# A convolution and joint network on one core: tap 0 loaded in halves of rows, a turned sample block copied out by two engines, the last group's lower rows stored in two column halves

## The chip, the cores and the metric

The kernel runs on one core of a Trainium2 chip. The metric is device time in microseconds (us): the median of several executions. One further execution was taken with the hardware profiler; every start and duration below is from it, counted from the first instruction of its span.

The core's engines, as the profile names them: PE (matrix products; PEld loads the weights of a product), DVE and ACT (vector and activation engine, which also copy results out of PSUM), POOL, and SP, which does no arithmetic and issues most DMA transfers. ACT issues a few. A "q" behind a name (SPq) means the engine's sequencer, which waits and issues.

## The reference

```python
# x (2, 4000, 512)  w1, w2 (5, 512, 512)  g (2, 8, 512)  w_f, w_g, w_o (512, 512), all bf16
def reference(x, w1, w2, g, w_f, w_g, w_o):
    B, T, D = x.shape
    K = w1.shape[0]
    pad = K // 2
    xp = jnp.pad(x, ((0,0),(pad,pad),(0,0)))
    h = jnp.zeros_like(x)
    for i in range(K):
        h = h + jnp.einsum("btc,cd->btd", xp[:, i:i+T, :], w1[i])
    h = _gelu(h)[:, ::2, :]
    ...                                  # the same again with w2: f, (2, 1000, 512)
    fe = jnp.einsum("btd,de->bte", f, w_f)
    ge = jnp.einsum("bud,de->bue", g, w_g)
    j = jnp.tanh(fe[:, :, None, :] + ge[:, None, :, :])
    return jnp.einsum("btud,dv->btuv", j, w_o)      # (2, 1000, 8, 512)
```

Two convolutions of five taps over time, each followed by gelu and by dropping every second sample; then a product with w_f, a sum with each of eight vectors per batch entry, tanh, and a product with w_o that gives 16,000 rows of 512.

## The kernel before

**Layout.** Channels lie on the 128 partitions in four chunks (index k, or c for the chunk of an input channel and m for the chunk of an output channel), samples along the free dimension. The samples of `x` lie in memory the other way round (a sample's 512 channels side by side), so they must be turned.

**Order of work.** Every operation (a group of matmuls, a copy, a DMA) is recorded in a plan, with the tiles that it reads and writes. Which engine does it, and in which order each engine does its own, stands in the strings of `ORDER`, written out by hand: two characters are one operation's number. `Plan.emit` then puts in the waits that the tiles demand. The numbers `cost`, `wire` and `nbytes` are a planner's estimates and change nothing in the program that runs. Each engine, SP too, works through its list strictly in order, so a waiting instruction holds all behind it.

**The first stage, up to about 23 us.** The outputs of the first convolution for the first 396 kept samples of batch entry 0 are computed directly, tap by tap, while the rest of the input is still on its way:
- `load_xr` (line 438) loads the first samples in two blocks, `xr[0]` of 128 rows and `xr[1]` of 72, each row holding four consecutive samples.
- `load_w1` (lines 430 and 456) loads the taps of w1. Taps 0 and 4 come in column halves `h` (output channels 0 to 255, and 256 to 511), taps 2, 1 and 3 whole. The order on SP is tap 0 first half, tap 4 first half, tap 0 second half, tap 4 second half, tap 2, tap 1, tap 3. A `gate` makes SP wait with a load until an earlier one has landed: tap 4's second half waits for `xr[0]`, tap 2 for `xr[1]`, tap 1 for the first half of tap 4, tap 3 for the second half of tap 4. Behind them on SP stand the transposing loads `load_x6` (line 445) of the other samples into `xq` and `xp`.
- While the loads run, PE does eight products with zeros (`warm_mm`). Then it turns the two blocks (line 489): for each block `rt` and each parity `pp` of the samples eight transposes into one PSUM bank, 4, 6, 5 and 7 in PE's order. DVE copies the banks of block 0 into `xs[0]` (line 496), ACT those of block 1 (line 404). On DVE the copy of the odd samples stands behind three sums over w1.
- `direct` (product of line 412) does, for a tap and an output chunk m, four matmuls, one for each input chunk k. The columns are 2 × 198 samples. The output chunks gather in PSUM banks 0 to 3. Taps go in the order 0, 4, 2, 1, 3; taps 0, 4 and 2 read even samples, taps 1 and 3 odd ones.
- `w1part` (DVE lines 398 and 500, ACT line 404) forms sums of taps, chunk by chunk of the outputs, for the units below. The first three on DVE read taps 0 and 4, the next tap 2. The tiles are `ssum`, `w_x` and `w_t`. In between, DVE and ACT form sums of samples (`row`) from `xq`.

**The units.** The rest of both convolutions goes in `Triple`s and `Unit`s: three outputs side by side from nine products of sums. Their first products are mixed into tap 3 of the direct stage on PE: the first output chunk of tap 3, then the first product of unit 1 (tile `row`, made by DVE, times `w_x`), the second chunk of tap 3, and so on.

**The joint stage.** After the convolutions, `Seven` handles four blocks of 128 output rows by seven products of half-size blocks in place of eight (`p1` to `p7`). Results gather in a tile `og` of four blocks by 512 columns: blocks 0 and 1 are the upper rows, 2 and 3 the lower. `block(r, c)` is half r of the rows and half c of the columns, 256 columns wide. Block (1, 1) is written by DVE in `p7`, block (1, 0) by ACT in `p4`, the upper blocks by DVE in `p2` and `p3`. `stores(r)` (line 932) stores both column halves of rows r in one DMA on SP, 256 KB in rows of 1 KB.

**The end.** For the last group, PE's order is p7, p2, p3, then the single block that is left over (`Plain`, two column halves of 64 KB, stored from ACT, line 830), then p4. On SP the last three issues are: the lower rows of the group before, the upper rows of the last group, its lower rows. Then SP waits for all stores.

Of the kernel before, what the change touches and what calls it, by code (L numbers as in the profile page):

```python
# [12 lines left out]
P = 128  # L13
# [50 lines left out]
class Op:  # L64
# [6 lines left out]
        "0Y0Z0a0b0c0d0e0f0g0i0k0m0u0v0w0x0y0z0_0-1011121314151617182D191h2d1A2w1B2K2L2n2o1j1k2f2g2F2G2y2z2q2r2N37382O34353P2k"  # L71
        "3Q313K2l3I323L3Y3u3V3i3j3W3S3f3T423w3a3b433x4Z4B4D4E4L3-3g45464M3l3m4b4c4O404I4p4g4m5M4J4j4k4P4n4w4x5W4z4r4_5q5X4s4h"
        "5O5P5T5U505s6M515_5Z5t5-6m6W6X5a6O6w6x6P6T5x5y7B796U61626o6p7J7K6Z7C7U6t7S6z6a7G7c7q7M6u7V7d7H7N6_7Z7s7t7f7g8U7a7_84"
        "817-827x8B8C8E7y86878F8n8e8o8s8W8H8X8f8b8I8u8v908p8q919E8h8z8c8_9G9H9L939R8i9S9M9U9V949g9O9p9P9r9i9w9zA49yA1A8AAAOA3"
        "9kAF9lAjAkAaAbACAIB2AxAyAJALB3AgBEAhBWBFAqAdArBXAeB8B9BZBLBMAMB5BaB6BlAtAuBcBdBSBTBrBBBOBsBCBPCIBfBuBvCCCFCGBgC9CAC2"
        "CDC3CmCUBiCJBjCVCLB_B-CbCpCqCXCYCnCcCMD6D7CsCvCtDGDKCfDLCwD3CgD4DWDdDCCyDeDXDNDODDDQDyDRDvCzDzDoDwDkDgDhDlDpDTDUEFEC"
        "EDE5EUE6E2D-EVE3EPE0EQEaEbEGEgELEuE-EvEMFDEXEYEdEeFEF0FPF3ExFGFHEyF5FJFsFtFkFXFyFRFMFYFKFaFbFzFNG8G9FvFwGLFgFhFmGMG2"
        "GBGCGFF-GGG0GUGOGZGVGRGSGfGuGgGPGXGoGvH1GiGpH4GjGxH2H6GyG_HZG-HNHCHyHTHOHzHDHUHFHGHbHhHiHQHWHXHqHRIZHrHJH-I0HKI2I3IC"
        "HkHlITIaIyIDI5IUIJI6IzIKIcIWIFIjIXIGIkJ2J3IdJPImJCJQJDIsJ5I-ItInJ0JJJ6JSJKJTJuJvJfJYJFJgJVJGJiJjJWJ_JZK8J-K9JxK1K2KN"
        "JyKTKUKOJoKFKWKGJpKXK_KQKBKCKdKeLLKmKRKuKvLRK-LMKnKxKgKhLSL8L9L1LFL2KyLULbLqLVLcLGLrLOLPLkLBLCMPLlMQMJMKLtM4LeLfM5Lz"  # L80
        "LuL_LwMmLxMnMZMaMMMSM7MNMBM8MTMCMpMsMtMqMgMhNHN0MvMcN1NIMdMwNmN3N4N7NKN8NNNLNnNONQNXNYOFNROGNaNsNeNfNbNvO0O1NtNpNqNw"
        "OVOWOLOMOOOiO3OjO4OPOIOJOoOyOzOpOrO7O8OsOlOmOcOYPCOdOZPFP9PAPGPDP3P4PIPaO-P0PbPSPPPQPJQ1PTQ2PjPkPgPdPhPePqPrPWPXQDQE"
        "PtQ4Q5PuPxPyQ7Q8QGQKQLQHQAQBQNQOQRQYQUQV"),
    "act": (
        "080l1M0n1p1O1z1S1r1R2T1Q2E1i2e1t1-1C1D1b2p2M1l1d1E1G2x1F2V392P2s2Y362X3R2Z2j2m3J3Z2J3v3C3k3o3U3E3X3330444C3p3q3h3O4N"
        "4a473n4T413e4q5N4l4Q3_4V4K4o544-5Y554i535r4v4y4H526N66604f6n5V706y5L6Y5b5S686V5w5K7A5z5p7L636S727T6b715o6L6v7e7I5i7O"
        "7k6s6-7r7w857h7Y6l7F807m8D7b6K838V7z8G8O8t8P6E8g6k8Q8J988A6e8a78929F8d8j9K8r8-9T9A959N9W8y9q9h9Q9j9_A59sAUA0APA7AVCk"
        "AlAHAEAWCiAKAYAXAZBGAsB1BNANBAC7B0C5BYBmBtC6BwA-CBClC4DJCWCjC8CZDICoDtDHDMDuD5F9ChETESDY9oC_FpDiFBCPF7F8FADsE7EEERFr"
        "EHEhEwGKFFFQF4EzFoFqGtGsFZFcFCHvGAFnHuG3INGJIwGhGYIRH5GkGwJNHwHPHEIQHHHxH_IPJsKrI4ISIEIVIxI_IOIbIlKsJEJRIoLoJOJwJhJk"
        "JtJXKLKAKVKJKqKKKfKMKwNiL0KiLTLALJLKLsLdMkMLLpM6KtLyMoMbMHM9MuMIMlMeNJNFNkNDNPN5NoNZOHNcNENlOXNjO5NGO_OhODOaOEPBOgP1"  # L90
        "PRPcPHQ3PUPsPiQFPvQ9QIQSQTQWQa"),
    "dve": (
        "000h1J1K1n0j1L1P1o1x1N1y1m1v1q2R1I2S1T1s1V1w1U1_1W1X1H1Y1Z1a1c1u202h1e2H2Q2_2U2-1f2I1g2i2W2u2a2c2b3M2t3N2v3D3A3B3r3c"
        "3F3d3G3y3z3s3H4F4G3t49484d4R4U4e4A4S4X564Y4W4t4u585d5e5Q57645c5F5u655H5I675v5R6B746c5l5G6Q6A5m5J6R6q6r6C6H69737D6I7E"
        "5j6D5h7R5k5g5n7Q757P7W7X6F6d6h7u7l7v6i776G7j6J7i6f7p887n6g897o6j8R8T8Y8S768w8Z8m8l978x96999I9X9b9J8k9f9Y9d9a9Z9B9t9u"
        "9x9v9-A29eABA6A99CAG9mAcAD9n9DAzA_B4AiAoAmAnATBHBpBIApAfBbB7AvBeBnBUBQBDBqC-CQBhCECHCKBkC0CrCdCNCODZDaEAD8CuEqDbCxDf"
        "DEDPDSD_DxDmDqDVEBDrEiEjElEWE4E1EcEnFTEoENEZF1EfFIF6EpFlFuFSFLFOF_FxFiGNGDGHG1GaGTGQI8HAH9HdGWGqH7GzH0HaH3HVHcHjHYHS"
        "HsHLI1HmI9IgJ8I7ILIYIHJ9IhJ4IeIuJ1J7JUJbK5JcJHJLJaK0K3JzKPKHJqKYKDKSKbL5M0KcLNKoLXL7KzLWLHLQLDL3LmLgLvL-MyM2MVM3MRMD"
        "MOMiMrN2MUMxN9NMNTNyNVNUORNzNSNgNrO2NxOkNuONOKOQO9OqOeOnPEP5OtPNOxPLPmPMPKPfPlPYQ6PzQMQCQPQZ"),
    "pool": (  # L100
        "010203040522210o0p0q0r0s0t5f8N9cASBJAQARBKCSBoD0D2CRD1CTDcErE8EsEtE9EkG4FUEmFWGbG6G5GcFVH8G7GdHeGeHgHBJAIAHfIfIiIBJB"
        "JdK4K7JeKZL4KaK6M1LYL6LZLaMXMWMzMYM_M-OSN_NWOTN-OuOUOvOwPnPOPoPp"),
    "sp": (
        "0607090A0B0C0D0E0F0G0H0I0J0K0L0M0N0O0P0Q0R0S0T0U0V0W0X232425262728292A2B2C595A5B5C5D5E8K8L8MAwBRBVBxByBzC1CaCeD9DADB"
        "DFDjDnEIEJEKEOE_F2FdFeFfFjGEGIGlGmGnGrHIHMHnHoHpHtIIIMIpIqIrIvJIJMJlJmJnJrKEKIKjKkKlKpLELILhLiLjLnMAMEMFMGMfMjN6NANB"
        "NCNdNhO6OAOBOCObOfP2P6P7P8PVPZPwP_P-Q0QJQQQX"),
# [178 lines left out]
def bass_standalone__seq2seq_rnn_t_joint__speech_kernel(  # L285
# [35 lines left out]
    with ExitStack() as es:  # L321
# [125 lines left out]
        came = [load_xr(rt) for rt in range(2)]  # L447
        act(warm[0:1], warm[1:2], ACT.Gelu_apprx_tanh)

        def load_w1(i, h=None, gate=None):  # L450
            src = w1[i].rearrange("(k c) d -> c k d", c=P)
            if h is None:
                o = load_w("sp", w1_sb[i], src)
            else:
# [9 lines left out]
        for i, h, gate in ((0, 0, None), (4, 0, None), (0, 1, None), (4, 1, 0), (2, None, 1), (1, None, 3), (3, None, 5)):  # L464
            load_w1(i, h, gate)
# [15 lines left out]
        for rt in range(2):  # L481
            for pp in range(2):
                bk, n = 4 + 2 * pp + rt, NR[rt]
                pv = View(psb[:, bk * 1024:(bk + 1) * 1024].rearrange("p (r k c) -> p r k c", r=2, k=NK)[:, :, :, 0:n], np.array([bk]), True)

                def fn(e, rt=rt, pp=pp, pv=pv, n=n):
                    for r in range(2):
                        for k in range(NK):
                            ins = e.transpose(pv.ap[:, r, k, :], xr[rt].h[0:n, 2 * r + pp, k, :], ident.h[0:n, 0:n])
                    return ins  # L490
                pl.op("pe", fn, (xr[rt].rows(0, n), ident[:]), (pv,), 0.55)
                o = xs[0][pp::2, :, 16 + rt * P:16 + rt * P + n]
                if rt:
                    act(o, pv, ACT.Copy)
                else:
                    pl.op("dve", lambda e, o=o, pv=pv: e.tensor_copy(out=o.ap, in_=pv.ap), (pv,), (o,), vec_cost(o, (pv,)))
# [180 lines left out]
        for i in taps:  # L677
            for m in range(NK):
                direct(i, m)
# [519 lines left out]
```

## Time and profile before

| what | us |
|---|---|
| the three runs | 249.5, 249.58, 250.33 |
| median of the runs | 249.58 |
| the profiled execution | 249.07 |
| its span, first to last instruction | 247.3 |
| first transpose, first direct product, first product of a unit (PE) | 4.57, 6.88, 18.82 |
| ACT's copy of the turned block of 72 rows, even samples | 6.17 to 6.82 |
| end of the last matmuls (PE) | 243.7 |
| last output copy (ACT) | 243.86 to 244.46 |
| last store issued (SP), landed | 244.48, 246.73 |

Busy shares of the span, from the profile's first part: PE 98%, PEld 75%, DVE 90%, ACT 86%, POOL 36%. The granted TensorE clock is 0.999 over the span. The DMA engines moved 31.85 MB, most of it in the first 30 us (loads) and the last 100 us (stores).

How to read it: a busy share is an average over stages. The chain of waits goes back from the last instruction, at each step to what released it; the timeline lists instructions in order of time; windows give the busy time and the DMA traffic of a stretch.

### The profile page before, as it was taken

The page shows a single profiled execution, that of the slowest core. Times are in us where ns is not written, and L with a number is a line of the kernel's source. Part 1 is how long each engine was busy: PE and PEld are TensorE (multiplying, and loading weights), DVE is VectorE, ACT ScalarE, POOL GpSimd, SP SyncE. Part 2 cuts the span into 40 slices and gives each one's busy share as a digit, 9 for nine tenths or more (in the row PEclk, how much of TensorE's full clock was granted, in tenths as well). Part 3 has the DMA queues.
Part 4 walks back from the last instruction along what each step waited for, and adds up shares of the span by engine and source line. Part 5 has one row for each costly group of instructions (what it writes and reads, how often), then busy time and mean ns, then how long its engine had stood idle before and what let it go on. Part 6 is the DMA issues. An engine that isn't in the chain of part 4 may idle for free.

```text
span 247.3 us, 5295 instructions
## 1 busy us (share of the span) xinstructions
PE 241.8 (98%) x1932; PEld 185.6 (75%) x1932; DVE 222.9 (90%) x394; ACT 212.0 (86%) x362; POOL 88.7 (36%) x94
## 2 busy tenths in 40 slices
PE   7999999999999999999999999999999999999994
PEld 4557788877666666666567887778778888888883
DVE  1699987987999998999898997999999999999993
ACT  2288899858777679986999999999999999999992
POOL 1000000000000000001054576578887786796970
PEclk9999999999999999999999999999999999999999
DMA  6999999985800150000000333313523555547457
GB/s 203 325 192 188 191 154 197 169 158 173 257 0 3 55 200 3 1 1 3 0 0 3 124 110 109 129 58 123 165 87 109 169 192 174 176 142 237 139 195 242
DMA packets 57851, 31.85 MB, mean 129 GB/s; under 512 B 33802, under 2 KB 57626, under 8 KB 57826
## 3 DMA queue, kind: packets, MB, share of 16 engines
q1 hardware_dynamic: 57538, 31.39, 48.7%
q8 instruction: 15, 0.25, 0.4%
q10 hardware_dynamic: 288, 0.13, 0.2%
q14 instruction: 10, 0.08, 0.1%
HBM read 7.64 MB, written 16.38 MB: 97 GB/s over the span
## 4 chain that ended last, share of the span: by engine, by line
PE 91%; DMA 6%; ACT 1%; SPq 1%; ACTq 0%; issue 0%
PE acc L412 91%; DMA xq<-in_x_dram 2%; DMA w_sb<-in_w_dram 2%; DMA xr<-in_x_dram 1%; SPq L445 1%; ACT row L404 0%; ACT og L815 0%; ACT w_x L404 0%; ACTq L830 0%; ACT ost L815 0%; SPq L430 0%; ACTq L246 0%
## 5 line engine op out<-in xcount | busy, mean ns | idle before, releaser
L398 DVE TENSOR_TENSOR og<-acc,sn 128x512 bf16<-128x512 f32 x93 | 60.0, 683 | 2.5 <-PE acc L412 1.8
L412 PE MATMUL acc<-tw,ss 128*128 128x256 f16 x372 | 57.8, 273 | 0.0
L404 ACT ACTIVATE jT<-feT,geT 128x1000 bf16<-128x1000 f32 (+6 forms) x56 | 54.3, 1017 | 0.3
L815 ACT ACTIVATE sn<-acc 128x512 f32<-128x512 f32 (+1 forms) x73 | 46.5, 725 | 0.7 <-PE acc L412 0.5
L412 PEld LDWEIGHTS acc<-tw,ss 128*128 128x128 f16 x372 | 36.3, 98 | 6.1
L412 PE MATMUL acc<-row,w_sb 128*128 128x334 bf16 (+1 forms) x192 | 32.0, 296 | 0.0
L884 POOL TENSOR_TENSOR ss<-jT 128x512 f16<-128x512 bf16 x22 | 25.6, 1174 | 13.9 <-ACT jT L404 13.4
L412 PE MATMUL acc<-row,w_x 128*128 128x268 bf16 (+1 forms) x192 | 29.1, 291 | 0.2 <-ACT w_x L404 0.2
L412 PE MATMUL acc<-wo_sb,jT 128*128 128x256 bf16 x176 | 29.0, 273 | 0.0
L404 ACT ACTIVATE sd<-acc 128x334 f32<-128x334 f32 (+1 forms) x48 | 20.4, 433 | 9.5 <-PE acc L412 9.3
L404 ACT ACTIVATE jX<-feT,geT 128x1000 bf16<-128x1000 f32 (+4 forms) x28 | 27.5, 1048 | 0.3 <-PE acc L412 0.3
L394 POOL MEMSET hT<- 128x8 bf16 (+2 forms) x6 | 0.6, 149 | 67.2 <-ACT hT L404 67.2
L412 PEld LDWEIGHTS acc<-row,w_sb 128*128 128x128 bf16 x192 | 18.7, 98 | 6.7 <-DVE acc L500 0.2
L412 PEld LDWEIGHTS acc<-row,w_x 128*128 128x128 bf16 x192 | 18.6, 98 | 6.6 <-ACT w_x L404 0.6
L412 PE MATMUL acc<-wo_sb,ss 128*128 128x256 bf16 x124 | 21.2, 273 | 0.0
L884 POOL TENSOR_TENSOR ss<-ss,jT 128x512 f16<-128x512 f16 x14 | 17.1, 1228 | 10.0 <-DVE ss L884 8.2
L412 PEld LDWEIGHTS acc<-wo_sb,jT 128*128 128x128 bf16 x176 | 17.2, 98 | 3.4
L884 POOL TENSOR_TENSOR ss<-jT,ss 128x512 f16<-128x512 bf16 x13 | 15.4, 1186 | 6.8 <-DVE ss L884 5.5
L404 ACT ACTIVATE hT<-acc 128x268 bf16<-128x268 f32 (+2 forms) x36 | 14.9, 432 | 2.8 <-PE acc L412 2.6
L412 PE MATMUL acc<-row,w_t 128*128 128x334 bf16 x96 | 16.9, 305 | 0.0
L815 ACT ACTIVATE og<-acc 128x512 bf16<-128x512 f32 x22 | 16.1, 731 | 0.9 <-PE acc L412 0.8
L412 PE MATMUL acc<-hT,w_sb 128*128 128x334 bf16 x96 | 16.6, 305 | 0.0
(115 smaller groups left out, 503.4 us busy)
## 6 DMA issues: line engine op xcount, KB each, us to landing
out_dram<-og SPq DMA_DIRECT2D x47, 256.0 KB, 2.2
w_sb<-in_w_dram SPq DMA_DIRECT2D x8, 512.0 KB, 4.8
out_dram<-og SPq DMA_DIRECT2D x15, 128.0 KB, 2.2
w_sb<-in_w_dram SPq DMA_DIRECT2D x4, 256.0 KB, 5.0
xr<-in_x_dram SPq DMA_DIRECT2D x1, 512.0 KB, 3.6
wf_sb<-in_w_f_dram SPq DMA_DIRECT2D x1, 512.0 KB, 3.6
wg_sb<-in_w_g_dram SPq DMA_DIRECT2D x1, 512.0 KB, 4.6
wo_sb<-in_w_o_dram SPq DMA_DIRECT2D x1, 512.0 KB, 3.6
```

Of the source, the lines that this page charges most:

```text
L394: pl.op("pool", lambda e: e.memset(v.ap, 0.0), (), (v,))
L398: pl.op(eng, lambda e: e.tensor_tensor(out=o.ap, in0=a.ap, in1=b.ap, op=op), (a, b), (o,), 0.02 + 2.14e-3 * o.ap.free_size() if eng == "po ...
L404: pl.op("act", lambda e: e.activation(o.ap, i.ap, func, scale=scale, bias=0.0 if bias is None else bias.ap), rd, (o,), o.ap.free_size() * ...
L412: ins = e.matmul(o.ap, lhsT=l.ap, rhs=r.ap, start=start and n == 0, stop=stop and n == len(pairs) - 1, skip_group_check=not check)
L445: pl.dma("sp", lambda e: e.dma_start_transpose(out=dst.ap, in_=src), (), (dst,), nbytes=n * 2 * D, rate=172e3)
L815: pl.flex({"act": (lambda e: e.activation(o.ap, v.ap, ACT.Copy), 0.05 + n * 0.833e-3), "dve": (lambda e: e.tensor_copy(out=o.ap, in_=v.ap) ...
L884: fn = lambda e, o=S[i], x=x, y=y, op=op: e.tensor_tensor(out=o.ap, in0=x.ap, in1=y.ap, op=op)
```

## The change

Three edits, and the strings of `ORDER` renumbered to match.

1. *Tap 0 in row halves.* Tap 0 of w1 is loaded as input chunks 0 and 1 (all 512 output columns), then input chunks 2 and 3; both come ahead of the two column halves of tap 4. Each part is 256 KB as before, now in rows of 1 KB. The list of gates keeps its places: tap 1's load now waits for the second part of tap 0. The direct products of tap 0 go in two passes over the four output chunks, first with input chunks 0 and 1, then with 2 and 3; the number of matmuls is the same.
2. *The turned block by two engines.* The even samples of the block of 72 rows are turned in two groups of four transposes, the first into bank 5, copied out by ACT, the second into bank 2, copied out by DVE, each 4 chunks × 72 = 288 elements. On DVE the copy of the odd samples of the block of 128 rows stands directly behind it, ahead of the three sums.
3. *The last store in column halves.* For the last group alone, `p7` stores block (1, 1) and `p4` block (1, 0), each 128 KB in rows of 512 B. On SP the new store stands between the lower rows of the group before and the upper rows of the last group.

Otherwise the order of operations on every engine is that of before.

```diff
         came = [load_xr(rt) for rt in range(2)]
...
-        def load_w1(i, h=None, gate=None):
+        def load_w1(i, part=None, gate=None):
...
-                sl = slice(h * D // 2, (h + 1) * D // 2)
-                o = pl.dma("sp", lambda e: e.dma_start(w1_sb[i, :, sl].ap, src[:, :, sl]), (), (w1_sb[i, :, sl],), nbytes=262144)
+                k, sl = part
+                o = pl.dma("sp", lambda e: e.dma_start(w1_sb[i, k, sl].ap, src[:, k, sl]), (), (w1_sb[i, k, sl],), nbytes=262144)
...
-        for i, h, gate in ((0, 0, None), (4, 0, None), (0, 1, None), (4, 1, 0), (2, None, 1), (1, None, 3), (3, None, 5)):
-            load_w1(i, h, gate)
+        lo, hi, al = slice(0, 2), slice(2, NK), slice(0, D)
+        for i, part, gate in ((0, (lo, al), None), (0, (hi, al), None), (4, (slice(0, NK), slice(0, D // 2)), None),
+                              (4, (slice(0, NK), slice(D // 2, D)), 0), (2, None, 1), (1, None, 3), (3, None, 5)):
+            load_w1(i, part, gate)
...
-        for rt in range(2):
-            for pp in range(2):
...
+        def turn(rt, pp, rs, bk):
+            n, k = NR[rt], len(rs)
+            pv = View(psb[:, bk * 1024:bk * 1024 + k * NK * P].rearrange("p (r k c) -> p r k c", r=k, k=NK)[:, :, :, 0:n], np.array([bk]), True)
+
+            def fn(e):
+                for i, r in enumerate(rs):
+                    for k in range(NK):
+                        ins = e.transpose(pv.ap[:, i, k, :], xr[rt].h[0:n, 2 * r + pp, k, :], ident.h[0:n, 0:n])
+                return ins
...
+        turn(0, 0, (0, 1), 4)("dve")
+        late = turn(0, 1, (0, 1), 6)
+        turn(1, 0, (0,), 5)("act")
+        turn(1, 0, (1,), 2)("dve")
+        late("dve")
+        turn(1, 1, (0, 1), 7)("act")
...
-        def direct(i, m):
-            mm(ps.cols(m * NT, 2 * NA), [(w1_sb[i, k, m * P:(m + 1) * P], both(i, k)) for k in range(NK)],
-               i == taps[0], i == taps[-1])
+        def direct(i, m, ks):
+            mm(ps.cols(m * NT, 2 * NA), [(w1_sb[i, k, m * P:(m + 1) * P], both(i, k)) for k in ks],
+               i == taps[0] and ks[0] == 0, i == taps[-1])
 
         for i in taps:
-            for m in range(NK):
-                direct(i, m)
+            for ks in ((range(2), range(2, NK)) if i == taps[0] else (range(NK),)):
+                for m in range(NK):
+                    direct(i, m, ks)
...
+            def store_half(self, r, c):
+                lo, t = (self.jt + 2 * r) * P, 2 * r
...
+                src = self.block(r, c)
+                pl.dma("sp", lambda e: e.dma_start(dst, src.ap), (src,), (), sem_of(("s", self.n % len(og), t)), 2 * P * 2 * H)
...
             def p7(self):
                 self.product(7, self.A, False)
                 self.out(1, 1, self.A, self.d5)
+                if self.n == len(jts) - 1:
+                    self.store_half(1, 1)
...
             def p4(self):
                 self.product(4, self.A, False)
                 self.out(1, 0, self.A, None, None)
                 free.append(self.A)
-                self.stores(1)
+                if self.n == len(jts) - 1:
+                    self.store_half(1, 0)
+                else:
+                    self.stores(1)
```

More of the change, by code (lines that the diff above doesn't have):

```diff
@@ L447, in bass_standalone__seq2seq_rnn_t_joint__speech_kernel @@
         came = [load_xr(rt) for rt in range(2)]
+        came[0].wire, came[1].wire = 1.74, 1.05
         act(warm[0:1], warm[1:2], ACT.Gelu_apprx_tanh)
-        def load_w1(i, h=None, gate=None):
+        def load_w1(i, part=None, gate=None):
             src = w1[i].rearrange("(k c) d -> c k d", c=P)
-            if h is None:
+            if part is None:
                 o = load_w("sp", w1_sb[i], src)
+                o.wire = 1.546
             else:
-                sl = slice(h * D // 2, (h + 1) * D // 2)
-                o = pl.dma("sp", lambda e: e.dma_start(w1_sb[i, :, sl].ap, src[:, :, sl]), (), (w1_sb[i, :, sl],), nbytes=262144)
+                k, sl = part
+                o = pl.dma("sp", lambda e: e.dma_start(w1_sb[i, k, sl].ap, src[:, k, sl]), (), (w1_sb[i, k, sl],), nbytes=262144)
+                o.wire = 0.74 if sl.stop - sl.start == D else 0.86
             if gate is not None:
@@ L932, in stores @@
                 pl.dma("sp", lambda e: e.dma_start(dst, src.ap), (src,), (), sem_of(("s", self.n % len(og), t)), 2 * P * 2 * NT)
+            def store_half(self, r, c):
+                lo, t = (self.jt + 2 * r) * P, 2 * r
+                vv = lo // T2
+                assert vv == (lo + 2 * P - 1) // T2
+                dst = out[vv // U, lo % T2:lo % T2 + 2 * P, vv % U, c * H:(c + 1) * H].rearrange("(t p) c -> p t c", p=P)
+                src = self.block(r, c)
+                pl.dma("sp", lambda e: e.dma_start(dst, src.ap), (src,), (), sem_of(("s", self.n % len(og), t)), 2 * P * 2 * H)
             def p1(self):
```

81 lines of the change are left out of this document (38 added, 43 removed).

## The prediction

> **What bounds the kernel now.** I read the chain of waits first. Its shares:
>
> ```profile
> PE 91%; DMA 6%; ACT 1%; SPq 1%; ACTq 0%; issue 0%
> ```
>
> Then the same chain in order of time (start, length, what):
>
> ```profile
> 0.74 3.60 DMA xr<-in_x_dram
> ...
> 4.35 4.78 DMA w_sb<-in_w_dram
> ...
> 9.55 1.37 SPq L445
> ...
> 10.97 6.08 DMA xq<-in_x_dram
> ...
> 17.07 1.10 ACT row L404
> 18.18 0.54 ACT w_x L404
> ...
> 18.82 224.06 PE acc L412 x1816
> ...
> 243.86 0.60 ACT og L815
> ```
>
> The reader is to see three stretches: loads up to 18.82 us, one unbroken run of matmuls to 242.88, and a drain to 247.3. Matmul starts after 18.82 are as far apart as their columns ask (about 0.109 us for 256, 0.114 for 268). Added up, PE loses only 0.27 us there, half of it near 27.4 and 28.3. So a microsecond taken ahead of 18.82, or out of the drain, reaches the end in full. One saved on PE before its stop at 18.82 does not.
>
> What sets 18.82? The timeline of DVE and PE (start, length, operation, count, idle before and its releaser):
>
> ```profile
> 6.88 11.69 PE L412 MATMUL acc<-xs,w_sb 128*128 128x396 bf16 x68 [0.48 <-ACT xs L404]
> 7.38 0.69 DVE L398 TENSOR_TENSOR ssum<-w_sb 128x512 f32<-128x512 bf16 x1 [1.46 <-DMA w_sb<-in_w_dram]
> 10.73 0.69 DVE L500 SCALAR_TENSOR_TENSOR ssum<-w_sb,ssum 128x512 f32<-128x512 bf16 x1 [0.85 <-DMA w_sb<-in_w_dram]
> 17.96 0.71 DVE L398 TENSOR_TENSOR row<-xq 128x1072 bf16<-128x1072 bf16 x1
> ```
>
> PE has done the direct products that it may do by 18.41 (the last of them starts at 18.24) and stands 0.41 us until 18.82. The next product, of unit 1, reads the `row` written by the DVE instruction of 17.96 (ends 18.67). DVE gets there without a gap from 10.73, twelve instructions 0.60 us apart, and at 10.73 it waited for the landing of w1[2], at 10.63. The page's chain names ACT's `w_x` of 18.08 instead, fed by a transposed load that landed at 17.05. Both lead back to the same queue: loads on SP run one behind the other, and the transposes are issued after the last w1 load, which waits for the fourth part to land (9.13). So the pace of the loads sets 18.82.
>
> **The front, step by step.** Landings in the trace: w1's four column parts of 256 KB (rows of 512 B) at 6.48, 7.36, 8.27 and 9.13, 0.88 us apart in the mean ((9.13 − 6.48)/3). The next loads, 512 KB each in rows of 1 KB, land at 10.63, 12.13 and 13.63: 1.50 apart, 0.75 for 256 KB. The windows agree: 293 GB/s at 5.6 to 8.2 us, 346 at 9.0 to 12.8.
>
> *Loads.* Tap 0's two parts become 256 KB each in rows of 1 KB. Two times 0.88 − 0.75 = 0.13: 0.26 us. Landings then: 6.34, 7.10, 8.00, 8.86, and w1[2] at 10.37. The gates of SP follow: the last w1 load is issued 0.26 earlier, and so are all transposes behind it. Bounds: 0 if rows of 512 B cost nothing here, 0.30 by the best pair of gaps (0.885 and 0.903 against 0.75).
>
> The Trainium skill speaks against this step. Its page "DMA: Bandwidth & Descriptors", section Specifications, puts transfers of 512 B and more at line rate, so that both row sizes would land alike and the 0.26 would be 0; this trace disagrees, with 0.88 against 0.75 us. The same page's section "Why small descriptors are slow (HBM only)" gives some 3 cycles per packet beside 16 for 512 B and 32 for 1 KB; the estimate from it is (19/16)/(35/32) = 1.09 and a saving near 0.13 us.
>
> *DVE.* Its first three sums (7.38, 8.00, 8.60) read tap 0 whole and tap 4's first part, now third in the queue: from 8.02 on, 0.60 us apart and the last 0.68 long, so they end near 9.91. The copy of the odd rows, now done in the hole before them (6.45 to 7.15), no longer stands between. The instruction of 10.73 goes at 10.47, 0.56 us after they end. That slack hides their delay; it is gone if tap 4's first part lands after 8.55. From 10.47 on the stream is unchanged, and `row` is ready 0.26 us earlier. Its transposed loads (14.52, 17.05) come earlier by as much.
>
> *The turned block.* The four transposes of one half take 4 × 0.033 = 0.13 us less than eight, so ACT starts at 6.04 instead of 6.17. Its copy of 288 elements is 0.65 − 288 × 0.84 ns = 0.41 (slope from its 256- and 512-element rows, 0.384 and 0.598). DVE's half starts at 6.17 and costs between 0.19 (its share of the 0.69 for 1024) and 0.45 (the 256-element f32 copy at 243.34 took 0.42); I take 0.28. Behind it on DVE stand the copy of the odd rows and the three sums, none due before 8.0. So the first product goes near 6.50 instead of 6.88 (6.43 to 6.68). The wait at 8.31 for the second column part (0.07 us) goes too, as tap 0's upper rows land at 7.10 and are first read 1.33 us after the start, at 7.83. PE gains 0.45 us here, and all of it runs into the stop for `row`: it arrives at 17.96 and waits until 18.56. Worth nothing by itself. The extra bank 2 is read out by 6.6; PE writes it as the third of four column groups, 0.67 us after its first product.
>
> Front: 0.26 us.
>
> **The drain.** The windows of DMA traffic (the last two columns are the engines' busy share and GB/s):
>
> ```profile
> 244.00:244.10 0.10, 0.00 (x0) 0.00 (x0) 0.00 (x0) 0.10 (x1) 0.00 (x0) 1.00 0.54 164
> 244.10:244.20 0.10, 0.00 (x0) 0.00 (x0) 0.00 (x0) 0.10 (x1) 0.00 (x0) 1.00 0.16 41
> 244.20:244.30 0.10, 0.00 (x0) 0.00 (x0) 0.00 (x0) 0.10 (x1) 0.00 (x0) 1.00 0.27 92
> 244.30:244.40 0.10, 0.00 (x0) 0.00 (x0) 0.00 (x0) 0.10 (x1) 0.00 (x0) 1.00 1.01 348
> ```
>
> The same view over the stretch behind the hole:
>
> ```profile
> 244.30:246.30 2.00, 0.00 (x0) 0.00 (x0) 0.00 (x0) 0.15 (x1) 0.00 (x0) 1.00 1.00 323
> ```
>
> The engines have a hole near 244.2, and then move everything left, without a pause, to 246.3: 256 KB issued at 243.34, two 64 KB from ACT (243.31, 243.88), and the last 256 KB issued at 244.48. That is 655 kB at 323 GB/s, 2.03 us. It lands at 246.73, and the closing steps end the span at 247.3.
>
> Bytes follow an issue by some 0.96 us (243.34 to 244.30). The new 128 KB store is issued by SP behind the one at 242.30 (0.39 long), at 242.70; its block was ready at 242.10. SP is free again near 243.2, ahead of 243.34, so nothing behind it waits. Its bytes are due at 243.66 and queue behind the 256 KB moving until 244.0. It fills the hole, 0.24 us at 323 GB/s being 78 kB, and pushes the rest back by what is left. The last store, now 128 KB, is issued at 244.48 as before and due at 245.45; the backlog lasts until about 245.7, so the bytes decide, not the issue. If row size cost nothing, the gain would be those 0.24 us. If rows of 512 B cost in stores what they cost in loads, the two halves pay 2 × (0.88/2 − 0.75/2), that is 0.07 for each 128 KB, 0.13 in all, and 0.11 is left. I take the middle, 0.17. Bounds: 0.38 at most (half of the last store at 344 GB/s, the window 245.4 to 246.2, with no backlog); a loss at worst, below.
>
> [...]
>
> **Sum.** 0.26 + 0.17 = 0.43 us. The profiled execution took 249.07 (span 247.3, and 1.77 around it): 248.64. The median of the runs, 249.58, lies 0.51 above it; I forecast from the median: 249.58 − 0.43 = 249.15, 249.1 rounded down for the profiled run's lower time.
>
> **Rivals** (0.3% is 0.75 us, about what a measurement of this kernel can tell from no change):
> - *Row size is no cost in this queue.* The 0.13 per part would then come from something else, such as the x block still arriving. For it: the first part's rows do overlap that block. Against: parts three and four do not, and were as slow. Front 0, drain 0.24: 249.34. Chance 0.10. The Trainium skill's line-rate rule, told above with its page, would make this case the true one.
> - *The drain is no shorter*: the hole closes but the later issue or the landing decides. For it: the last issue stays at 244.48. Against: a saturated queue to 246.3. Only 0.26: 249.32. Chance 0.15.
> - *The first product decides after all*: if `row` came early enough, PE's 0.45 would count. Against it: DVE's gapless stream. 0.45 + 0.17: 248.96. Chance 0.10.
> - *Slower*: stores in rows of 512 B run badly. The place is the drain, where two halves of 128 KB replace rows of 1 KB. Each costs 0.38 us at 344 GB/s now; the slowest row of the windows just before is 143 GB/s (242.9 to 243.0, other stores on the engines), by which each would take 0.92: 2 × 0.54 − 0.24 = 0.84 lost. Less the front, 0.58: 250.16; with no front, 250.42. It decides from where a half takes 0.25 us more, below about 208 GB/s. Against it: ACT's two 64 KB stores have 512 B rows and moved in a stretch of 325 GB/s (244.3 to 245.2, the mean of its windows). Chance 0.15.
>
> **How the numbers follow.** The forecast itself has 0.50. Faster by over 0.3% needs 0.75, which front (0.30) and drain (0.38) at their bounds just miss; the third rival and the scatter of runs (249.07 to 250.33) give it 0.25. Slower by over 0.3% needs the fourth rival with no front, or scatter: 0.10. Within 0.3%: 0.65. Range: the bounds together, 249.58 − 0.68 = 248.9, and the rivals to 249.4, widened by 0.3 to 0.4 for scatter: 248.6 to 249.8. It leaves out the fourth rival.
>
> **What would show it.** First product near 6.50 and no stop near 8; landings 0.75, then 0.88 apart; the DVE instruction of 10.73 near 10.47, PE's run from 18.56 with a longer wait, now about 0.6; no hole in the traffic near 244 and the last landing near 0.43 earlier. It is wrong if tap 4's first part comes after 8.55, if new stops of PE appear between 19 and 40 us, or if the last two stores move at much under 300 GB/s.

## The result and the profile after

The kernel after took 248.85 us in the median of 21 runs (248.54 to 249.72), the kernel before 249.45 in 21 runs beside it (248.81 to 250.33). The ratio is 0.998, interval 0.9971 to 0.999: 0.5 us less, between 0.25 and 0.72. The forecast was 0.43 less, or 249.1 in time; 0.13 of the 0.25 us between that and 248.85 comes from its start, 249.58, the median of the three runs known then. The profiled execution took 248.66 (before 249.07), its span is 246.83 (247.27).

The chain of waits of the kernel after, in order of time (start, length, what):

```profile
0.74 3.27 DMA xr<-in_x_dram
4.02 4.70 DMA w_sb<-in_w_dram
9.15 1.64 SPq L445
10.84 6.44 DMA xq<-in_x_dram
17.30 1.11 ACT row L404
18.41 0.00 issue
18.41 224.04 PE acc L412 x1816
...
243.43 0.60 ACT og L831
```

It has the same three stretches. The matmuls take 224.04 us in place of 224.06, so nothing was won or lost in them; their run begins 0.41 earlier, at 18.41 in place of 18.82. Between landing and span end the difference of the two traces adds up as follows: tap 2 lands 0.40 earlier (10.23 for 10.63), the last matmul starts 0.02 sooner after that landing, and the end comes 0.02 sooner after the last matmul: 0.44, the difference of the spans. The 0.40 is almost all in the first w1 part, which landed at 6.10 in place of 6.48; the three parts behind it land 0.86 to 0.91 us apart in both traces. So the first sign that the prediction named, a gap of 0.75, isn't to be seen in this execution.

The timeline of DVE and PE in the kernel after (start, length, operation, count, idle before and its releaser), the counterparts of the instructions of 7.38, 10.73, 17.96, 6.88 and 18.82 before:

```profile
6.68 1.00 PE L412 MATMUL acc<-xs,w_sb 128*128 128x396 bf16 x5 [0.15 <-DVE xs L503]
7.89 0.69 DVE L398 TENSOR_TENSOR ssum<-w_sb 128x512 f32<-128x512 bf16 x1 [0.69 <-DMA w_sb<-in_w_dram]
10.32 0.69 DVE L515 SCALAR_TENSOR_TENSOR ssum<-w_sb,ssum 128x512 f32<-128x512 bf16 x1 [0.53 <-DMA w_sb<-in_w_dram]
17.55 0.71 DVE L398 TENSOR_TENSOR row<-xq 128x1072 bf16<-128x1072 bf16 x1
18.41 0.62 PE L412 MATMUL acc<-row,w_x 128*128 128x268 bf16 x4
```

The reader is to see the stream of DVE: the instruction that waits for tap 2 starts 0.41 earlier, with 0.53 us of slack ahead of it, and `row` follows 7.23 us behind, as before. The product of unit 1 starts 0.15 behind the end of `row` (18.26). The page's chain of the kernel before named ACT's `w_x`. ACT's instruction of that place, in the timeline of the kernel after:

```profile
18.31 0.61 ACT L404 ACTIVATE w_x<-ssum 128x512 bf16<-128x512 f32 x1
```

It was still running, until 18.92, when PE had begun at 18.41. So it isn't what holds the unit. The chain of the kernel after names ACT's own `row` in that place, which ends at 18.40; that is coincidence, since in cols_first (below) the same instruction ends at 19.36 and the unit has begun at 19.12. In twelve of the fourteen traces below the unit starts 0.145 to 0.147 us behind the end of DVE's `row`, and in the two others PE itself comes later. So DVE's `row` is what holds it.

### The profile page after: what moved, and what is told of

Its sections match the earlier page's. It is cut to its first block, busy times and chain, and to the rows that moved or that the text cites. A ratio compares the mean times of both kernels' runs of the same rounds, so it can differ in the third digit from the quotient of the medians.

```text
span 246.8 us, 5296 instructions
## 1 busy us (share of the span) xinstructions
PE 241.8 (98%) x1932; PEld 186.1 (75%) x1932; DVE 223.1 (90%) x395; ACT 211.6 (86%) x362; POOL 88.7 (36%) x94
## 4 chain that ended last, share of the span: by engine, by line
PE 91%; DMA 6%; ACT 1%; SPq 1%; ACTq 0%; issue 0%
PE acc L412 91%; DMA xq<-in_x_dram 3%; DMA w_sb<-in_w_dram 2%; DMA xr<-in_x_dram 1%; SPq L445 1%; ACT row L404 0%; ACT og L831 0%; ACTq L846 0%; ACT ost L831 0%; SPq L430 0%; ACTq L246 0%
```

## The experiments

The ratios are to the kernel before, run beside each, whose medians in the three later sets of runs were 249.15, 249.1 and 249.07. A ratio's interval is some 0.001 to 0.0015 to each side, 0.25 to 0.4 us, as large as the terms in question, so the stamps of the traces carry most verdicts. All in us; "first part" is the landing of the first 256 KB of w1, "unit" the start of the first product of unit 1, "law" the last matmul's start less tap 2's landing, "end" the span's end less the last matmul's start.

| kernel | ratio | first part | tap 2 | unit | last matmul | law | end |
|---|---|---|---|---|---|---|---|
| before | | 6.48 | 10.63 | 18.82 | 243.47 | 232.83 | 3.81 |
| after | 0.998 | 6.10 | 10.23 | 18.41 | 243.04 | 232.81 | 3.79 |
| before_again | 0.9995 | 6.42 | 10.63 | 18.81 | 243.44 | 232.81 | 3.81 |
| e1_rows_only | 1.0001 | 6.32 | 10.37 | 18.55 | 243.51 | 233.15 | 3.83 |
| e2_turn_only | 0.9992 | 6.49 | 10.67 | 18.86 | 243.52 | 232.85 | 3.81 |
| e3_stores_only | 0.9994 | 6.48 | 10.66 | 18.95 | 243.78 | 233.12 | 3.73 |
| after_again | 0.9992 | 6.53 | 10.40 | 18.58 | 243.24 | 232.84 | 3.72 |
| cols_first | 1.0002 | 6.83 | 10.89 | 19.12 | 244.03 | 233.14 | 3.69 |
| rows_all | 0.9993 | 6.15 | 9.86 | 18.48 | 243.42 | 233.56 | 3.83 |
| xr80 | 0.9991 | 7.53 | 11.42 | 19.61 | 244.23 | 232.81 | 3.77 |
| front_both | 0.9989 | 6.36 | 10.39 | 18.82 | 243.29 | 232.90 | 3.80 |
| store_late | 0.9996 | 6.18 | 10.22 | 18.56 | 243.04 | 232.82 | 3.99 |
| rows_only_again | 1.0011 | 6.89 | 10.86 | 19.27 | 245.02 | 234.16 | 3.83 |
| rows_all_again | 0.9982 | 6.23 | 10.02 | 18.47 | 243.30 | 233.28 | 3.75 |

My theory: the landing of tap 2 paces everything up to the drain. The rivals are those of the prediction, and, for the first edit, that the order of the parts and not their row size makes the gain.

### The kernel before against itself

No edit.

> The kernel before, unchanged, to see what of the two traces is scatter. In the trace of before the first x block landed at 4.33 us and tap 2 at 10.63; in that after the change 4.01 and 10.23. Row-size theory (the prediction): the x block is as it was by chance or not at all tied to the change; parts of tap 0 and 4 again 0.88 apart, tap 2 landing 10.63 within 0.1, first unit product 18.8. Chance theory (the early landing of the x block after the change was luck of one execution): here the x block may land anywhere from 4.0 to 4.35 and the first unit product moves with it, 18.4 to 18.8. Time: ratio 1.000 to the kernel before.

Measured: 0.9995 (0.998 to 1.001), median 249.23. Its first x block landed at 4.04, in the kernel before at 4.33, and tap 2 landed at 10.63 in both. So the landing of that block is chance, and tap 2's doesn't hang on it. Its first direct product went at 7.19, 0.31 later than in the kernel before, and its unit at 18.81 all the same. The scale follows too: one such comparison doesn't resolve 0.3 us.

### Edit 1 alone: tap 0 in row halves

```diff
-        for i, h, gate in ((0, 0, None), (4, 0, None), (0, 1, None), (4, 1, 0), (2, None, 1), (1, None, 3), (3, None, 5)):
+        for i, part, gate in ((0, (lo, al), None), (0, (hi, al), None), (4, (slice(0, NK), slice(0, D // 2)), None),
+                              (4, (slice(0, NK), slice(D // 2, D)), 0), (2, None, 1), (1, None, 3), (3, None, 5)):
...
+            for ks in ((range(2), range(2, NK)) if i == taps[0] else (range(NK),)):
```

> Only tap 0's loads and products in row halves; the turned block and the last store as before. Row-size theory: tap 0's two parts land 0.75 apart, tap 2 at 10.37 with the x block at 4.33; the copy of the odd samples still stands behind the three DVE sums and ends near 10.3, so the next sum starts at 10.4 to 10.5; first unit product 18.55; time -0.2 to -0.3 us. Early-block theory (fewer packets behind the x block let the block itself land earlier, the gaps between parts stay 0.87): x block 4.0, tap 2 near 10.23, first unit product near 18.5; time -0.3 to -0.4 us. Chance theory: x block anywhere between 4.0 and 4.35, the gain of this kernel by itself near 0.

The same kernel once more:

> Tap 0's row halves alone, once more. In its first trace the first unit product came at 18.55, as the landing of tap 2 asked, but PE lost 0.33 us more than the other kernels near 37 us, and the ratio was 1.000 (0.998 to 1.002). If that loss was of that one execution: no stop beyond 0.05 us near 37 here, first unit product to last matmul 224.63 to 224.67, ratio 0.998 to 0.9995. If it belongs to the edit without the turned block: the same 0.3 us again. Cover theory: with the first direct product late (6.9 to 7.1) PE's wait ahead of the unit is only 0.1 us or none, where both edits leave 0.05 to 0.3.

Measured: 1.0001 (0.9984 to 1.0017) and 1.0011 (1.0002 to 1.002), medians 249.38 both. In the first execution the front did what was forecast: tap 2 landed at 10.37, the unit began at 18.55 (18.56 was forecast). That it came to the hundredth is luck, as such landings scatter by more; tap 0's two parts were 0.79 apart, not 0.75, and in the second execution tap 2 landed at 10.86. And yet nothing reached the end: the last matmul starts 233.15 us after that landing, 0.32 more than before. PE of this kernel near 37 us:

```profile
35.73 0.28 PE L412 MATMUL acc<-xq,w_t 128*128 128x268 bf16 x1
36.85 0.63 PE L412 MATMUL acc<-row,w_sb 128*128 128x268 bf16 x4
37.56 0.62 PE L412 MATMUL acc<-row,w_x 128*128 128x268 bf16 x4
```

PE stands 0.10 us ahead of the second and 0.24 ahead of the third, where the kernel before loses 0.04 in all. DVE of the same kernel:

```profile
36.35 0.45 DVE L504 SCALAR_TENSOR_TENSOR acc<-acc,sd 128x268 f32<-128x268 f32 x1 [1.04 <-PE acc L412]
36.71 0.71 DVE L398 TENSOR_TENSOR row<-row 128x1072 bf16<-128x1072 bf16 x1
```

and the first of these in the kernel before:

```profile
36.31 0.45 DVE L500 SCALAR_TENSOR_TENSOR acc<-acc,sd 128x268 f32<-128x268 f32 x1 [0.74 <-PE acc L412]
```

In the kernel before it starts 0.04 behind the end of the product that the trace names as its releaser (36.27), here 0.34 behind (36.01): DVE idles 0.30 us longer, and the front's gain is gone. The second execution, 250.64 long and so 1.3 over its median, shows the same place and size: that instruction at 37.87, 0.35 behind its releaser and with DVE idle for 1.06, PE stops of 0.11 and 0.24 at 38.37 and 39.07. (Beyond that its transposed loads were late, the second landing at 18.38, and PE has a stop of 0.65 at 23.75, for a `row` of DVE.) No other kernel of the study has it. What holds the instruction, no view shows; it stays open.

### Edit 2 alone: the turned block by two engines

```diff
+        turn(0, 0, (0, 1), 4)("dve")
+        late = turn(0, 1, (0, 1), 6)
+        turn(1, 0, (0,), 5)("act")
+        turn(1, 0, (1,), 2)("dve")
+        late("dve")
+        turn(1, 1, (0, 1), 7)("act")
```

> Only the turned block in two groups for ACT and DVE, with the copy of the odd samples ahead of the sums. By the prediction: the first direct product 0.2 to 0.4 us earlier, the stop ahead of the first unit product longer by as much, that product where tap 2's landing puts it (18.8 if tap 2 lands at 10.63): time 0.0. The rival that the first product decides: first unit product and end 0.2 to 0.4 us earlier.

Measured: 0.9992 (0.9977 to 1.0007), median 249.14. Tap 2 landed at 10.67, the unit began at 18.86, 8.18 behind it as in the kernel before, and PE stood 0.41 for it. Alone the edit is worth nothing that the trace shows. But the first direct product went at 6.88, as before, and not 0.2 to 0.4 earlier: eleven of the block's transposes started 0.107 us behind the one ahead (none before; see the last section). So this trace doesn't test what an earlier first product is worth.

### Edit 3 alone: the last store in column halves

```diff
             def p7(self):
...
+                if self.n == len(jts) - 1:
+                    self.store_half(1, 1)
...
-                self.stores(1)
+                if self.n == len(jts) - 1:
+                    self.store_half(1, 0)
+                else:
+                    self.stores(1)
```

> Only the last group's lower rows stored in two column halves. By the prediction: the hole in the DMA traffic near 244.2 is gone, the last landing 0.17 us earlier (0.11 to 0.24) counted from the last matmul: time -0.17. By the trace after the change (counted from the last matmul the last landing came only 0.03 earlier): the two halves move at about 285 GB/s, the gain 0.0 to 0.1 us.

Measured: 0.9994 (0.9976 to 1.0011), median 249.25. The end comes 3.73 behind the last matmul, 3.81 before: 0.07 gained, not 0.17. (Its unit was 0.10 late in that execution, as the second transposed load landed at 18.06; before, 17.05.)

### The kernel after again

No edit.

> The changed kernel once more. Tap 2 landed at 10.63 to 10.67 in four traces with column parts (whether the x block landed at 4.04 or 4.33), at 10.37 with row parts alone and at 10.23 in the trace after the change. Row-size theory: here 10.23 to 10.40, first unit product 8.2 us behind that landing, 18.4 to 18.6; the last landing 3.2 us behind the last matmul. Chance theory: 10.6 as well as 10.2. Time: ratio 0.998 again (0.997 to 0.999).

Measured: 0.9992 (0.9982 to 1.0002), median 248.83: 0.2 us less, between 0.45 less and 0.05 more. Tap 2 at 10.40, the law 232.84, the end 3.72.

### Column parts in the new order

All of the kernel after, but tap 0 in column halves, both ahead of tap 4's, and its products in one pass again.

```diff
-        for i, part, gate in ((0, (lo, al), None), (0, (hi, al), None), (4, (slice(0, NK), slice(0, D // 2)), None),
-                              (4, (slice(0, NK), slice(D // 2, D)), 0), (2, None, 1), (1, None, 3), (3, None, 5)):
+        for i, h, gate in ((0, 0, None), (0, 1, None), (4, 0, None), (4, 1, 0), (2, None, 1), (1, None, 3), (3, None, 5)):
```

> The changed kernel with tap 0 in its old column halves (rows of 512 B), both ahead of tap 4 as after the change, and tap 0's products in one pass; the turned block and the last store as after the change. It parts the size of the rows from the order of the loads. Row-size theory: tap 2 lands at 10.6 to 10.7 again, first unit product at 18.8, nearly all of the gain gone: ratio 0.999 to 1.000. Order theory (what counts is that tap 0 is whole before tap 4): tap 2 lands at 10.2 to 10.4, the gain stays: ratio 0.998.

Measured: 1.0002 (0.9991 to 1.0014), median 249.04. Tap 2 landed at 10.89. Its DVE and PE:

```profile
10.98 0.69 DVE L509 SCALAR_TENSOR_TENSOR ssum<-w_sb,ssum 128x512 f32<-128x512 bf16 x1 [0.41 <-DMA w_sb<-in_w_dram]
18.26 0.72 DVE L398 TENSOR_TENSOR row<-xq 128x1072 bf16<-128x1072 bf16 x1
19.12 0.27 PE L412 MATMUL acc<-row,w_x 128*128 128x268 bf16 x1 [0.22 <-DVE row L398]
```

The parts landed 0.90, 0.92 and 0.84 apart. The order is that of the kernel after and the gaps are those of column parts again: it is the row size, and not the order, that sets them. The time agrees (249.04, beside 248.83 in after_again), but the intervals of the two ratios overlap; and part of the late tap 2 is this execution's first part, which landed at 6.83. (In this execution, too, the second transposed load was late, 18.23, and held `row` back a little.)

### All four parts in rows of 1 KB

```diff
-        for i, part, gate in ((0, (lo, al), None), (0, (hi, al), None), (4, (slice(0, NK), slice(0, D // 2)), None),
-                              (4, (slice(0, NK), slice(D // 2, D)), 0), (2, None, 1), (1, None, 3), (3, None, 5)):
+        for i, part, gate in ((0, (lo, al), None), (0, (hi, al), None), (4, (lo, al), None),
+                              (4, (hi, al), 0), (2, None, 1), (1, None, 3), (3, None, 5)):
...
-            for ks in ((range(2), range(2, NK)) if i == taps[0] else (range(NK),)):
+            for ks in ((range(2), range(2, NK)) if i in taps[:2] else (range(NK),)):
```

> The changed kernel with tap 4 in row halves too, so that all four parts have rows of 1 KB (tap 4's products in two passes like tap 0's). Row-size theory: another 2 x 0.13 us, tap 2 lands at 10.0 to 10.1; the three DVE sums now wait for the fourth part, near 8.5, and end near 10.4, so DVE's next sum comes at 10.4 and most of the step is lost again: first unit product 18.4 to 18.5, time as after the change within 0.1 us. If row size does not matter: tap 2 lands as after the change (10.2 to 10.4) and the sums end near 10.6, first unit product 18.6 to 18.7.

The same kernel once more:

> All four parts in rows of 1 KB, once more. First trace: gaps between the parts 0.75, 0.74, 0.73, tap 2 at 9.86, but the first unit product at 18.48, behind a second transposed load that landed at 17.59. If DVE's sums hold it (they wait for the fourth part): next sum 1.83 us behind the landing of the fourth part, first unit product 8.2 to 8.3 us behind that sum's start. If the transposed load holds it: the row sum starts at that landing. Time within 0.1 us of the change, ratio 0.999.

Measured: 0.9993 (0.998 to 1.0006) and 0.9982 (0.9966 to 0.9997), medians 249.0 and 248.64. All gaps are 0.71 to 0.75, and tap 2 lands at 9.86 and 10.02. But the last matmul follows 233.56 and 233.28 after that. The first execution's DVE and ACT:

```profile
10.20 0.69 DVE L515 SCALAR_TENSOR_TENSOR ssum<-w_sb,ssum 128x512 f32<-128x512 bf16 x1
17.61 0.72 DVE L398 TENSOR_TENSOR row<-xq 128x1072 bf16<-128x1072 bf16 x1
```

```profile
17.61 1.10 ACT L404 ACTIVATE row<-xq 128x1080 bf16<-128x1080 bf16 x1 [0.86 <-DMA xq<-in_x_dram]
```

The instruction for tap 2 no longer waits for its landing: the three sums ahead of it must have all of tap 4 now and end only at 10.20. Then the transposed load takes over: it lands at 17.59, and both engines' `row` start 0.02 behind it. So of the earlier landing, 0.2 to 0.5 us against the kernels with tap 0 alone in rows (10.22 to 10.40 in most), little reaches the end. Whether it beats the kernel after isn't settled: its two ratios and that kernel's two (0.998, 0.9992) overlap.

### The second x block with 80 rows

All of the kernel after; the block of 72 rows is loaded with 8 more, which nothing reads.

```diff
-            n = NR[rt]
+            n = -(-NR[rt] // 16) * 16
```

> The changed kernel with the second x block loaded with 80 rows of samples in place of 72 (the last eight are not used). The Trainium skill (DMA: Bandwidth & Descriptors, section on why a DMA increments its semaphore by 16) states that a DMA is split over the largest number of engines up to 16 that divides its slowest dimension: 12 for 72 rows, 16 for 80. If the engines with the most to do set the landings, each then has 20 KB of that block in place of 24 KB, 4 KB less at 16 KB per 0.75 us: all landings of the parts and of tap 2 about 0.19 us earlier, first unit product 0.19 earlier unless the second transposed load (17.28 after the change, against 17.55 for the sum that reads it) holds it. If the total traffic sets them: 32 KB more at 340 GB/s, 0.1 us later.

Measured: 0.9991 (0.9978 to 1.0005), median 248.88, no different from the kernel after. Its profiled execution, 249.8, had the first w1 part at 7.53, a microsecond late, so its landings don't tell whether the rows spread better; inconclusive. Two things it does show. With everything 1.2 us late, the law is 232.81. And the block's landing is counted in 16 steps (5.02 to 5.56 us) with 80 rows, in 12 (5.30 to 5.66) with the 72 of the kernel before: the engine counts that the expectation started from are right, only what they are worth stays open.

### Edits 1 and 2, the last store whole

The kernel after without the new stores; the edit is that of edit 3, taken out.

> The first two edits (tap 0 in row halves, the turned block on two engines) with the last store whole as before. So far the first unit product came 8.18 us behind the landing of tap 2 in eight traces of ten, and where it came later the second transposed load had landed late. Row-size theory: tap 2 lands at 10.2 to 10.4, first unit product at 18.4 to 18.6, the last landing 3.27 behind the last matmul; time -0.25 to -0.4 us, ratio 0.9985 to 0.999, that is nearly the whole of the change. If the last store is worth 0.17 us after all: only half to two thirds of the change's gain.

Measured: 0.9989 (0.998 to 0.9997), median 248.87. Tap 2 at 10.39, the end 3.80 behind the last matmul as before. Its PE and DVE:

```profile
4.57 2.70 PE L492 MATMUL acc<-ident,xr 128*128 128x128 bf16 x32
7.37 0.34 PE L412 MATMUL acc<-xs,w_sb 128*128 128x396 bf16 x1
10.48 0.69 DVE L513 SCALAR_TENSOR_TENSOR ssum<-w_sb,ssum 128x512 f32<-128x512 bf16 x1 [0.53 <-DMA w_sb<-in_w_dram]
17.72 0.71 DVE L398 TENSOR_TENSOR row<-xq 128x1072 bf16<-128x1072 bf16 x1
18.82 0.62 PE L412 MATMUL acc<-row,w_x 128*128 128x268 bf16 x4
```

The 32 transposes take 2.70 us (before: 1.82, with a wait of 0.23 in them), the first direct product goes at 7.37 instead of 6.88, and PE comes to the unit at 18.82, without a wait. `row` was there at 18.43; with the 0.15 behind it that before and after both show, 18.58 was possible, so PE is 0.24 late. Still the last matmul starts 232.90 after tap 2, 0.07 more than before. The rest PE had back by 28.4: the stops of 0.12 and 0.05 us that before has at 27.37 and 28.34 aren't there.

### The new store behind the upper rows

All of the kernel after; on SP the issue of the first half store changes places with that of the upper rows (one swap in SP's string of `ORDER`).

```diff
-        "NINjNnOCOGOHOIOhOlP8PCPDPEPbPfQ0Q4Q5Q6QPQTQXQe"),
+        "NINjNnOCOGOHOIOhOlP8PCPDPEPbPfQ0Q4Q5Q6QPQXQTQe"),
```

> The changed kernel with the new half store moved on SP behind the store of the upper rows, so that the same rows of 512 B are stored but the hole in the traffic is not filled. In ten traces the last landing came 3.27 us behind the last matmul with the whole store and 3.14 to 3.27 (mean 3.21) with the halves. If the 512 B rows cost what the gain lacks (0.24 for the hole, 0.06 gained, 0.09 for each half): last landing 3.40 to 3.50. By the prediction's 0.07 for each half: 3.40. If rows of 512 B cost nothing and the hole was worth only 0.06: 3.27.

Measured: 0.9996 (0.9987 to 1.0004), median 249.08. Its windows of DMA traffic (the last two columns are the engines' busy share and GB/s):

```profile
243.70:243.80 0.10, 0.00 (x0) 0.00 (x0) 0.00 (x0) 0.10 (x1) 0.00 (x0) 1.00 0.04 10
...
245.00:245.90 0.90, 0.00 (x0) 0.00 (x0) 0.00 (x0) 0.00 (x0) 0.00 (x0) 1.00 1.01 289
```

and those of the kernel after:

```profile
243.70:243.80 0.10, 0.00 (x0) 0.00 (x0) 0.00 (x0) 0.10 (x1) 0.00 (x0) 1.00 0.93 246
...
245.10:245.70 0.60, 0.00 (x0) 0.00 (x0) 0.00 (x0) 0.00 (x0) 0.00 (x0) 1.00 0.95 283
```

The hole is back (busy share 0.04), and the last landing comes 3.44 behind the last matmul. In the seven traces with halves and no hole it comes 3.21 behind in the mean (3.14 to 3.27), in the six with one whole store 3.27 (3.26 to 3.28). So closing the hole is worth 3.44 − 3.21 = 0.23, and the two halves cost 3.44 − 3.27 = 0.17 against one store in rows of 1 KB. Both rest on this one trace; only the net, 0.06, is from the thirteen others. The rate agrees: 283 and 289 GB/s, where the whole store moved at 344; 262 kB take 0.91 us in place of 0.76, 0.15 more.

## Why the prediction was right, and where it wasn't

**The front's 0.26: the mechanism is right, and half of the size is shown.** In the five traces with column parts, tap 2 lands 4.06 to 4.21 us after the first part, mean 4.16; in the seven with tap 0 in rows 3.87 to 4.14, mean 4.00: 0.16 for the one part in that stretch whose rows grew, 0.13 forecast. With all four parts in rows the stretch is 3.71 and 3.80, another 0.25, for two parts. So 0.12 to 0.16 for each part, and cols_first excludes the order. The rival "row size is no cost" falls, and with it, here, the line-rate rule that the prediction quoted from the Trainium skill's page "DMA: Bandwidth & Descriptors".

The other 0.13, for the first part itself, isn't resolved. It lands at 6.48 by columns and 6.36 by rows in the median, but at 6.54 and 6.56 in the mean: it scatters from 6.10 to 6.89 with the same row size (and 7.53 in xr80). The kernel after drew the earliest of the seven, and so the 0.40 of its profiled execution is mostly chance: its gap to the second part was 0.87, where the six others with tap 0 in rows show 0.77 to 0.80. What made that gap long, and what scatters the first landing, is open. The time of front_both, 0.27 us less (0.07 to 0.5), holds 0.16 as well as 0.26.

**"The pace of the loads sets 18.82": right, and more tightly than forecast.** In eight of fourteen traces the last matmul starts 232.81 to 232.90 after tap 2 lands, whatever became of the product before it. The reason is more than the unit. DVE works without a gap from tap 2 on, and in the kernel before its stream gives PE two more tiles late:

```profile
26.63 0.68 DVE L398 TENSOR_TENSOR w_t<-ssum,w_sb 128x512 bf16<-128x512 f32 x1
27.58 0.70 DVE L398 TENSOR_TENSOR row<-row 128x1072 bf16<-128x1072 bf16 x1
```

They end at 27.31 and 28.28, and PE's two stops, 0.12 at 27.37 and 0.05 at 28.34, are the waits for them. So DVE's stream, counted from the landing, sets PE once more near 28 us, and up to 0.17 us of lateness of PE at the unit is made good there. The prediction saw these stops, but not what they were.

The six other traces have further waits: a late second transposed load (17.6 to 18.2) in e3_stores_only, cols_first and both rows_all, the DVE instruction near 37 in both runs of edit 1 (and a late transposed load in the second). In the first four the law is 0.29 to 0.73 over 232.83, of which the unit's own delay is 0.05 to 0.43; the rest goes in stops of PE behind it, most of them between 22 and 28 us, for DVE's `row` and `w_t` or ACT's `sd`.

One sentence failed in the profiled execution: "its transposed loads come earlier by as much". The second landed at 17.28, later than the 17.05 of before, though it was issued 0.13 earlier (10.84 for 10.97). This landing scatters too, from 16.66 to 18.38 with tap 0 in rows and from 17.05 to 18.23 in columns. It didn't matter here, as `row` on DVE was due at 17.55. With another 0.4 us off tap 2's landing it did, in rows_all. So the transposes are what is late next.

**The turned block: sizes right, place wrong.** ACT's half copy took 0.41 as forecast, DVE's 0.31 (0.28). But the first direct product went at 6.68, not 6.50, and at 7.10 in after_again and 7.37 in front_both. The term that failed is the transposes: I took the block of 128 rows to be turned as fast as in the trace of before; there the sixteen of the block of 128 rows start 0.056 us apart, in the kernel after the first eight 0.107 apart, in after_again, front_both and store_late all sixteen. So PE's wait for `row` is not 0.6 but 0.30 us, 0.05 in after_again and none in front_both and store_late. In rows_all_again, where the transposes ran at full pace from their start at 4.39, the first product went at 6.47 and the wait was 0.56. "Worth nothing by itself" agrees with the time of e2_turn_only, though the first product was no earlier there. But in executions like front_both and store_late PE is late already, and without what the edit saves it would be later still; how much of that would stand at the end isn't shown, since in front_both PE made good 0.17 of 0.24. That edit 1 alone gave nothing may belong here, but e1_rows_only had PE waiting 0.15 for `row`, which speaks against it. The runs show only that edits 1 and 2 together gave 0.9989 (0.998 to 0.9997) and edit 1 alone 1.0001 and 1.0011, and where that was lost.

**The third rival, "the first product decides": no.** PE's own lateness moved the last matmul by 0.07 of 0.24 us in front_both (232.90 for 232.83) and not at all in store_late (0.16 late, 232.82). Before_again says the same: the first product 0.31 later, the unit at 18.81 for 18.82.

**The drain's 0.17: mis-sized, 0.06.** By store_late the hole was worth what I said, 0.23 (0.24). The step that failed is the cost of the 512 B rows: "what they cost in loads", 0.07 for each half, of which I then took half. It is 0.086 for each, 0.17 in all; even the full loads' price of 0.13 was too little. The rival "slower", stores in rows of 512 B at under 208 GB/s, falls at 283 and 289. "The drain is no shorter" (0.15) came closer than my forecast. The Trainium skill's page "DMA: Bandwidth & Descriptors", section "Rules for kernel authors", says not to bother with two transfers to disjoint partition halves, since both share the same engines. The halves here are of columns, so no run here tests that. What these runs show is another account: an early half fills a hole, worth 0.23, and the two pay 0.17 for their rows.

**The sum.** The front has 0.16 that is shown and 0.12 more by the medians of the first landing, the drain 0.06: the change is worth 0.22 to 0.34 us. Both measurements of it, 0.25 to 0.72 less and 0.45 less to 0.05 more, hold that. The forecast of 0.43 had 0.11 too much for the drain; that it came so near the 0.5 of the first measurement is in part luck, as the second gave 0.2.

## What to carry to other kernels

Where loads run one behind the other and the compute stream hangs on the last, find the landing that the end keeps a constant distance to, over several executions. A gain there reaches the end only as long as that distance holds, which it did not in edit 1 alone nor with all parts in rows, and single executions differ by more than the gain. Splitting a transfer pays only what the hole in the traffic is worth less what the shorter rows cost; take both from windows of the same direction, as here the loads' price was too low for stores. An edit that shortens the path can give nothing alone, and something beside another that is worth nothing alone (why, these runs don't show): run each alone and both together.

## What the runs showed of the hardware

- Transposes at half pace. Of the sixteen of the first block, none starts 0.107 us behind the one ahead in the kernel before, seven do in the kernel after, all fifteen in front_both and store_late; the others start 0.056 apart. Before_again, the same program as before, has eleven of them, so it is the execution and not the kernel. It is the clock: each trace keeps a record of the granted clock, which begins, at full clock, between 4.19 and 6.93 us (4.59 in the kernel before, 5.34 in the kernel after, 6.93 in front_both). In twelve traces it begins in the very step in which the pace changes, in the two others (e3_stores_only, rows_all_again) ahead of the first transpose, and there none is slow. The windows read 1.00 throughout because they count the time ahead of the record as full. The Trainium skill's page "TensorE: Matmul & The Clock Gate", section "Part 1: The HAM clock gate (the "warmup" mystery)", puts the start-to-start time of such a product at 106.7 ns with a cold array and 55.6 with a warm one, and says that the moment of the change wanders with the phase of a window of 3.4 us. These traces agree with the two times and show the moment wander; the record of full clock lasts 242.35 us in thirteen of them and 238.93 in front_both, 3.41 less.
- The landing of a block's 72 rows is counted in 12 steps, that of 80 or 128 rows in 16.
- The landing of the first w1 part, 6.10 to 7.53 us with the same row size, while the first x block's landing (3.96 to 4.33) has no bearing on it.
- Stores from rows of 512 B at 283 to 289 GB/s where rows of 1 KB moved at 344; loads at 0.84 to 0.92 us for 256 KB (column parts alone) against 0.71 to 0.75 (row parts alone).
- A DVE instruction that started 0.34 and 0.35 us behind its releaser in the two runs of one kernel, 0.04 in the kernel before, with nothing visible to hold it.
